# Score matmuls over whole 128-key chunks in 32x128 array tiles, barred squares cleared after the exponential, and a new order of the work

## The chip, the cores and the metric

The kernel runs on one core of a Trainium2 chip. A core has a matrix engine (TensorE, PE in the profile; PEld is its weight load), a vector engine (VectorE, DVE), a scalar engine (ScalarE, ACT), a general engine (GpSimd, POOL) and an engine for issuing transfers (SyncE, SP). Each engine works through its own list of instructions in order; semaphores order them against each other. The metric is device time in microseconds of one execution; lower is better.

## The reference

Attention with a block-causal mask, followed by one MLP-mixer layer. Inputs are q, k and v of shape (8, 8, 576, 64): eight batches, eight heads, 576 positions, head dimension 64. Cut to what matters:

```python
scores = scale * np.matmul(q, k.transpose(0, 1, 3, 2))
mask = block_i >= block_j                       # blocks of 64 positions
scores = np.where(mask, scores, -1000000000.0)
attn = softmax(scores)                          # over the keys
attn_out = np.matmul(attn, v)
x = attn_out.transpose(0, 2, 1, 3).reshape(B, S, 512)
h = np.maximum(x.transpose(0, 2, 1) @ w_tok1, 0.0) @ w_tok2     # over positions: 576 -> 256 -> 576
u = x + h.transpose(0, 2, 1)
h2 = np.maximum(u @ w_ch1, 0.0) @ w_ch2                         # over channels: 512 -> 1536 -> 512
out = u + h2
```

A query in block i sees the keys of blocks 0 to i, nine blocks of 64 in all. The kernel computes in bfloat16 with float32 accumulation.

## The kernel before, in words

**Scores.** Queries and keys are loaded as bfloat16 and transposed on VectorE as 32-bit pairs (line 442), so the 64 numbers of a head lie as two parities of 32 partitions. Four heads (a head group, `hg`) fill the 128 partitions, 32 each. A score matmul of one head therefore contracts over 32 rows, twice (`par` 0 and 1), and the array is used as tiles of 32 rows: four heads at once, one in each row group. Scores are made transposed, keys on the output partitions, queries along the columns. For each batch and head group there are three sets (`SETS`, emitted by `score_set`, matmuls at line 569), each of which fills one PSUM bank of 512 columns per head: set 0 holds key blocks 4 to 8, set 1 key blocks 2 and 3 and one square of blocks 0 and 1, set 2 the rest of blocks 0 and 1. Each entry of `SETS` is one matmul per head: (half of the output partitions, key block, first query block, first column, columns, parity). Before the change every matmul has 64 keys, so each row group holds two 32x64 tiles, one for each half of the partitions.

**The bar.** A chunk of 128 keys is two blocks. Queries of the first block may see the first 64 keys but not the second 64: a barred square of 64 keys by 64 queries. Before the change three of these squares (one in set 0, two in set 1) are written by a matmul of a constant tile `bar` (minus 2.5e8 times 1, entries with key block `None`), whose exponential is zero. Key block 8 stands alone and is copied to `et_sb` by `tail` (line 595); `tail` then clears the place that it left in `e_sb`, which is the barred square of blocks 6 and 7 (line 600).

**After the scores.** ScalarE takes the exponential of each bank into `e_sb` (line 776; lines 587 and 737 for batch 0). `head_out` (line 617) multiplies it with the values, which carry a column of ones for the sums; `ends_out` (line 670) does the last query block of two heads at a time in 128x64 tiles; VectorE divides. Then token mixing (lines 811, 815, 910; for batch 0 line 846), and the channel products up and down (1038 and 1460 for batch 0, 1111, 1235 and 1369 for the others, which trade matmuls for sums on VectorE). Results leave PSUM through VectorE or ScalarE (lines 395, 397, 797, 799, 925, 1393 and others).

**The order.** Each piece of work is an operation with a number, the number in which `Plan.add` was called. The constant `ORDER` lists all of them, in the order in which they are emitted; a letter names the engine (T TensorE, A ScalarE, D VectorE, P GpSimd, S SyncE), and small letters after T the PSUM banks that the operation takes. So each engine's list, the choice between VectorE and ScalarE or GpSimd, and the banks are all written out by hand; the costs given to `Plan.add` do not act here. GpSimd issues the loads (lines 419, 437, 471, 482, 505, 514) from the same list in which it copies and clears; SyncE issues the stores and the transposing loads of u (line 977).

**The start.** `raise_clock` issues 11 matmuls on zeros (line 366) and then small fillers on zeros (line 373) wherever `ORDER` names them; fillers that it does not name are not emitted. Batch 0's scores use two double banks (`sc`) that later become the four banks `late`.

Of the kernel before, what the change touches and what calls it, by code (L numbers as in the profile page):

```python
# [10 lines left out]
BF16 = mybir.dt.bfloat16  # L11
# [16 lines left out]
class Plan:  # L28
# [69 lines left out]
    16S 0A 11D 10D 13S 9D 21P 1D 2D 43Ta 5D 19P 4D 3D 23P 33P 27P 14A 25P 31P 15D 29P 17A 20D 37P 44Tb 45Tb 46Tb 22D  # L98
    47Ta 36P 48Ta 49Ta 18D 50Ta 51Ta 52Ta 35P 53Ta 24D 54Ta 55Ta 56Ta 125Ts 34P 100Ttbc 179P 126A 28D 57Ta 58Ta 59Ta
    176P 60Ta 61Ta 26D 62Ta 101A 12P 106Ts 63Ta 32D 182P 64Ta 107A 65Ta 104Tt 42P 30D 66Ta 67Ta 105A 68Ta 39P 123Ts  # L100
    102D 103D 69Ta 70Ta 41P 119A 71Ta 157Tt 124A 112Td 40P 113T 116Ta 108Tb 114D 120A 38P 109T 115D 138Ts 158A 181D
    81P 72Td 73Tc 74Tc 121D 75Tc 122D 139A 82P 76Tc 7D 144Tt 110D 111D 84P 135Td 178D 127Tc 145A 161Ts 185P 136D
    117D 137D 140D 131Tb 180D 83P 128T 162A 142Tt 177D 90P 132T 129D 143A 77Td 89P 163Ts 130D 133D 86P 134D 78Td
    164A 118D 141D 159D 200Tdcba 160D 85P 203A 173Te 154Tf 165Tg 202A 91P 174D 166T 155D 156D 201A 184D 92P 205Tbhfc
    204A 183D 169Td 88P 170T 209A 167D 263Ta 168D 208A 175D 150Tc 171D 261Tg 172D 207A 187D 267Td 206A 87P 186D
    146Te 262A 147T 264A 151T 268D 237Tgbfh 152D 339P 6D 148D 269Ta 153D 241A 149D 273Td 189P 240A 270D 281Tc 239A
    274D 265Te 190P 238A 271Ta 8D 282D 275Tb 266A 191P 193Tdhfg 276A 272D 283Te 196A 277Tc 342P 194A 315Ta 278D
    306Tb 197A 188P 294Td 195A 279Tc 284A 192P 318Tf 198D 280D 291Tg 319T 348P 316T 309Tc 317A 310T 257D 93P 320A
    307T 295T 94P 308A 292T 311A 258D 225Teahf 345P 296A 300Tb 227A 95P 285Tc 228A 286T 293D 226A 303Td 287D 229A
    304T 351P 232Tahge 341D 199D 312Tc 230D 233A 305D 313T 234A 231D 288Tf 344D 314A 297Ta 340D 236A 289T 343D 235A  # L110
    210Td 513P 245Tc 290A 211D 213Th 516P 212D 242Te 246D 216Tg 354P 247D 301T 214D 215D 248Td 243D 302A 298T 244D
    355P 217D 219Tc 249D 299A 250D 222Th 220D 254Te 221D 363Tdbaf 255D 256D 251Tc 349D 364A 330Te 352P 252D 365A
    218D 253D 321Td 367A 223D 224D 366A 259D 353P 368Tcghb 420Ta 372A 370A 422Tb 347D 371A 525P 346D 322T 421D 423A
    260D 369A 356Tafgh 323T 359A 357A 350D 424Tb 360A 324D 331T 358A 425D 388Tcadg 361P 514D 430Tb 391A 434Th 332T
    389A 431D 435A 518D 426Td 392A 517D 400Thcbf 390A 515D 428Tg 404A 393P 362D 334Ta 522P 403A 429D 677P 401A 335T
    333D 402A 528P 427D 376Tb 373Tc 394D 527P 96D 395Tdfgh 379Te 526P 377D 396A 374D 336T 375D 397A 519P 378D 380D
    405Tc 398A 680P 381D 382Tb 399A 406D 385Td 407D 432Te 337D 417Tc 383D 386D 433A 530Tafgh 387D 384D 418D 436Td
    419D 531A 440Tb 97D 414Tc 534A 325Te 533A 98D 326T 532A 415D 437A 416D 542Tahgf 99D 441A 438Tc 545A 327T 439D
    544A 444D 463Tgd 543A 445D 448Thb 328D 466A 464Tc 451D 546A 329S 411Ta 408Te 465A 446D 469T 412D 690P 413D 449Tf
    523D 470A 454T 529P 450A 409D 442Ta 410D 452Tc 455A 443D 691P 467Tg 520D 453A 537Taefh 447D 692P 468A 456T 521D  # L120
    538A 473T 689P 524D 539A 471T 679D 540A 683P 596Ta 457D 541A 474D 562Tcefh 597A 678D 458T 566A 681D 594Ta 565A
    459D 564A 460D 476T 563A 595D 461T 477A 569Tchfe 682D 462A 472D 604Ta 847P 571A 478Tdb 475D 686P 572A 605D 602Tg
    535P 481A 600Th 603D 536P 570A 598Ta 567P 482Tf 601D 607S 568P 553Tc 844P 599D 483A 479Tg 550Th 554D 555D 480A
    488T 551D 484T 552D 606S 489D 486T 485A 556Tc 487D 491T 573A 574Thadg 557D 490D 492A 547Te 558D 577A 493D 497Tbf
    575A 548D 576A 549D 559Tc 578A 688D 701Tedah 498A 685D 579Tg 560D 704A 684D 499T 705A 494D 850P 702A 693P 580D
    585Ta 703A 581D 503T 500D 687D 706Tgdbh 586D 587D 561D 591Te 504D 710A 501Ta 709A 495D 708A 592D 707A 593D 582Tc
    502D 627Tbd 612The 608D 630A 588Tg 583D 496D 505T 859P 615D 858P 633T 584D 506D 507T 857P 634A 589D 590D 860P
    694Tcgab 508D 856P 618T 698A 849D 509T 697A 846D 696A 619D 695A 760Tb 609D 610D 699P 510D 738Tacgh 761A 848D
# [42 lines left out]
    1457D 1392D 1492The 1453D 1393T 1488D 1493A 1489D 1455D 1498T 1394D 1458T 1396S 1460T 1490D 1459D 1472Tca 1468D  # L171
    1465S 1461D 1494T 1464S 1473A 1469D 1476Td 1470D 1478T 1491D 1462T 1479D 1471D 1499D 1482T 1463D 1496Tg 1477D
    1466S 1483D 1502T 1467S 1497D 1484T 1503D 1500T 1507S 1485D 1495D 1480T 1487S 1501D 1474T 1506S 1481D 1504T
    1475D 1486S 1505D 1508S
"""


@with_exitstack
def kernel(
# [340 lines left out]

    BARRED = 2.5e8

# [1057 lines left out]
```

## Time and profile before

| | |
|---|---|
| median of three runs | 284.23 us (284.23 to 285.07) |
| the profiled execution's own time (its span; the page gives no other) | 284.7 us |
| TensorE busy, instructions | 275.8 us, 4038 matmuls |
| VectorE, ScalarE, GpSimd busy | 240.3, 180.4, 71.7 us |
| instructions of line 569: loads of keys, loads of the bar | 1280, 192 |

In the profile a line names the engine, the source line and the operation, what is written and read, and the shape. For matmuls the shape begins with the array tile (rows * columns). TensorE's matmuls are pipelined: a matmul's listed duration includes its way through the array, and the next one starts before it ends, so what a matmul costs is the distance to the next start. A time in brackets is the engine's idle time before the instruction, with what ended it; "issue" means that nothing the profile shows was waited for.

### The profile page before, as it was taken

Reading aid. Unit: us, or ns where it says so; the run is one execution under the profiler, and the core shown is the slowest. Engines: PE = TensorE matmul, PEld = TensorE weight load, DVE = VectorE, ACT = ScalarE, POOL = GpSimd, SP = SyncE. Lnnn points to the kernel's source line nnn. Section 1 sums busy time; section 2 is a strip of 40 time slices with the busy share of each in tenths; the row PEclk is TensorE's granted clock in tenths of the full one; section 3 lists DMA queues with packets and bytes.
Section 4 is the critical chain, followed back from the end, with each engine's and each line's share of the span. In section 5 each row is a group of like instructions: output and inputs, shape, how many; then the busy total and the mean of one; then the engine's idle time right before and its main releaser. Section 6 shows DMA issues by size and latency. Waiting matters only on the chain.

```text
span 284.7 us, 9438 instructions
## 1 busy us (share of the span) xinstructions
PE 275.8 (97%) x4038; PEld 197.6 (69%) x4038; DVE 240.3 (84%) x519; ACT 180.4 (63%) x325; POOL 71.7 (25%) x120
## 2 busy tenths in 40 slices
PE   7998999999999899999999999999999999999994
PEld 3667656556878676987777658744488876468883
DVE  3589569799999799999998997997998987598893
ACT  3798685778888358996879785136546653764000
POOL 8975635170641062060341220000000000000000
PEclk9999999999999999999999999999999999999999
DMA  8999999969989495898199587130033403000246
GB/s 160 166 174 202 190 205 203 137 94 134 144 120 119 71 84 87 225 135 122 11 169 102 87 106 132 49 119 18 2 74 98 126 7 131 12 2 0 104 127 212
DMA packets 64776, 31.79 MB, mean 112 GB/s; under 512 B 53088, under 2 KB 55904, under 8 KB 64736
## 3 DMA queue, kind: packets, MB, share of 16 engines
q0 software_dynamic: 45040, 17.64, 53.1%
q1 hardware_dynamic: 19696, 13.57, 19.6%
q8 instruction: 31, 0.51, 0.7%
q14 instruction: 9, 0.07, 0.1%
HBM read 35.85 MB, written 9.44 MB: 159 GB/s over the span
## 4 chain that ended last, share of the span: by engine, by line
PE 92%; DVE 2%; ACT 2%; DMA 1%; issue 1%; SPq 0%; DVEq 0%
PE late L1369 14%; PE mm L1369 11%; PE late L1235 7%; PE mm L1111 7%; PE late L1111 6%; PE mm L569 6%; PE mm L1235 6%; PE mm L617 4%; PE mm L811 3%; PE mm L910 3%; PE mm L1038 3%; PE late L569 2%; PE late L617 2%; PE late L811 2%; PE mm L1460 2%; PE late L1460 2%
## 5 line engine op out<-in xcount | busy, mean ns | idle before, releaser
L776 ACT ACTIVATE e_sb<-late 128x512 bf16<-128x512 f32 x89 | 50.5, 609 | 10.4 <-PE late L569 9.1
L776 ACT ACTIVATE e_sb<-mm 128x512 bf16<-128x512 f32 x79 | 45.1, 609 | 9.9 <-PE late L569 6.6
L471 POOL DMA_DIRECT2D vals<-in_v_dram x45 | 37.2, 844 | 26.7 <-PE late L617 15.9
L442 DVE STREAM_TRANSPOSE qk_sb<-qk_sb 128x288 int32<-128x288 int32 (+2 forms) x57 | 36.2, 694 | 4.6 <-ACT qk_sb L395 3.5
L1369 PEld LDWEIGHTS <-sums 128*128 128x128 bf16 x288 | 27.6, 98 | 5.6 <-issue 1.8
L1369 PEld LDWEIGHTS <-gT 128*128 128x128 bf16 x288 | 27.8, 98 | 4.6
L569 PEld LDWEIGHTS <-qk_sb 32*64 32x64 bf16 x1280 | 19.9, 104 | 13.1 <-issue 8.8
L569 PE MATMUL mm<-qk_sb 32*64 32x64 bf16 (+7 forms) x546 | 27.8, 291 | 0.0
L569 PE MATMUL late<-qk_sb 32*64 32x512 bf16 (+7 forms) x594 | 27.1, 291 | 0.0
L617 PEld LDWEIGHTS <-e_sb 128*128 128x128 bf16 x640 | 23.8, 97 | 4.1 <-issue 0.9
L1111 PEld LDWEIGHTS <-ws_sb 128*128 128x128 bf16 x192 | 17.8, 98 | 3.4 <-issue 1.3
L797 ACT ACTIVATE gT<-mm 128x512 bf16<-128x512 f32 x25 | 14.7, 601 | 7.8 <-PE mm L1111 3.0
L617 PE MATMUL mm<-vals,e_sb 128*128 128x65 bf16 x430 | 19.0, 193 | 0.0
L643 DVE TENSOR_TENSOR x_sb<-mm,rinv 128x256 bf16<-128x256 f32 x43 | 17.9, 421 | 1.1
L1111 PEld LDWEIGHTS <-wc_sb 128*128 128x128 bf16 x144 | 15.4, 114 | 1.8 <-issue 0.2
L1235 PEld LDWEIGHTS <-ws_sb 128*128 128x128 bf16 x96 | 9.3, 98 | 10.1 <-issue 0.2
L1369 PE MATMUL late<-wd_sb,sums 128*128 128x256 bf16 x108 | 13.6, 272 | 1.2 <-issue 1.2
L1369 PE MATMUL late<-wd_sb,gT 128*128 128x256 bf16 x120 | 14.7, 273 | 0.0
L595 POOL COPY vals<-e_sb 128x256 bf16<-128x256 bf16 x10 | 4.1, 412 | 40.9 <-issue 22.9
L395 ACT COPY mm<-late 128x512 f32<-128x512 f32 x17 | 9.9, 584 | 7.1 <-PE late L1235 5.0
L797 ACT ACTIVATE gT<-late 128x512 bf16<-128x512 f32 x17 | 10.2, 602 | 6.3 <-PE late L1235 3.4
L1235 PE MATMUL late<-e_sb,ws_sb 128*128 128x512 bf16 x44 | 12.6, 379 | 0.0
(203 smaller groups left out, 656.2 us busy)
## 6 DMA issues: line engine op xcount, KB each, us to landing
out_dram<-o_sb SPq DMA_DIRECT2D x14, 512.0 KB, 3.1
vals<-in_v_dram POOLq DMA_DIRECT2D x28, 128.0 KB, 5.4
qk_sb<-in_k_dram POOLq DMA_DIRECT2D x12, 288.0 KB, 6.3
qk_sb<-in_q_dram POOLq DMA_DIRECT2D x12, 288.0 KB, 5.9
out_dram<-o_sb SPq DMA_DIRECT2D x7, 256.0 KB, 3.2
wc_sb<-in_moe_w_ch_dram POOLq DMA_DIRECT2D x8, 192.0 KB, 7.7
wc_sb<-in_moe_w_ch_dram POOLq DMA_DIRECT2D x3, 512.0 KB, 10.4
vals<-in_v_dram POOLq DMA_DIRECT2D x15, 64.0 KB, 4.9
```

The lines of the kernel that those rows point to most:

```text
L442: nc.vector.transpose(dst[:, 0:S, :] .rearrange("p s e -> p (s e)") .bitcast(I32) .rearrange("p (a k) -> p k a", k=NB)[:, k0:k1], raw2.bit ...
L471: nc.gpsimd.dma_start(out=t[128 - p : 128, J, hs, 0:64], in_=src)
L569: nc.tensor.matmul(out=home(n)[64 * half : 64 * half + 64, c : c + w], lhsT=bar[r, 0] if j is None else kT[i][r, 64 * j : 64 * j + 64, par ...
L617: nc.tensor.matmul(out=u[:, I, 0:65], lhsT=e[:, h, c : c + 128], rhs=vt[:, J, head, 0:65], start=(J == 0), stop=(J == I),)
L643: nc.vector.tensor_tensor(out=xt[:, 0:4, 64 * head : 64 * head + 64], in0=u[:, :, 0:64], in1=ri[:, 0:4].to_broadcast([128, 4, 64]), op=MULT,)
L776: nc.scalar.activation(dst, bank_of(x), EXP, scale=scale)
L797: nc.scalar.activation(dst, src, RELU)
L811: nc.tensor.matmul(out=ps, lhsT=w1_sb[:, c, tt : tt + 255 : 2], rhs=xt[:, c, cols], start=(c == 0), stop=False)
L1111: nc.tensor.matmul(out=bank_of(bank)[:, 256 * o_ : 256 * o_ + 256], lhsT=x(o_, m), rhs=y[:, :, m, :], start=opens, stop=m == 1, skip_group ...
L1235: nc.tensor.matmul(out=bank_of(bank), lhsT=x(m), rhs=y[:, :, m, :], start=first and m == 0, stop=m == 1, skip_group_check=not first,)
L1369: nc.tensor.matmul(out=bank_of(bank)[:, 256 * i : 256 * i + 256], lhsT=x[:, kk, 128 * i : 128 * i + 128], rhs=y[:, kk], start=first and i ...
L1460: nc.tensor.matmul(out=ps, lhsT=gT[0][:, cc, 128 * si : 128 * si + 128], rhs=wc2_sb[:, cc, :], start=cc == 0, stop=cc == NDC - 1,)
```

## The change

1. Sets 1 and 2 use whole chunks of 128 keys: entries with half `None` write all 128 partitions, in 32x128 tiles. A set of four heads has 16 matmuls for 32 (set 1) and 8 for 16 (set 2).
2. Set 0 keeps 32x64 tiles. Its wide pair now has the same 320 columns for key blocks 4 and 5 and its parts change places; 40 matmuls for 44.
3. The tile `bar`, its two memsets and its matmuls go. The barred squares come out as real scores, and their exponentials are zeroed: `clear` sets two squares of 64 keys by 64 queries to zero with one memset, for set 0 (there one of the two is the place that `tail` left, as before) and for set 1. `head_out` and `ends_out` wait for the clears. There are 36 clears for 18.
4. The fillers of `raise_clock` become 512 columns wide, every fourth 256; 28 are in the order, for 35.
5. `ORDER` is new throughout, and with it banks and engines; the first loads on GpSimd and SyncE keep their places among each other.

```diff
 ORDER = """
-    16S 0A 11D 10D 13S 9D 21P 1D 2D 43Ta 5D 19P 4D 3D 23P 33P 27P 14A 25P 31P 15D 29P 17A 20D 37P 44Tb 45Tb 46Tb 22D
...
+    7D 5D 14S 19P 41Ta 17P 48Tb 3D 21P 58Tb 31P 25P 23P 29P 27P 53Tb 51Tb 0A 15A 6D 11S 35P 56Tb 12A 74Tb 55Tb 2D 9D
...
-    bar = sb.tile([128, 2, 64], BF16, name="bar")
...
-        fill("DVE", "bar", -1e5 + 1, (bar[:, 0, :], -BARRED), (bar[:, 1, :], 1.0))
...
         for n in range(KEEP):
             bank = {"covers": False}
-
-            def emit(o, bank=bank):
+            w = 512 if n % 4 else 256
+
+            def emit(o, bank=bank, w=w):
                 nc.tensor.matmul(
-                    out=bank_of(bank)[:, 0:256], lhsT=zeros[:, 0:128], rhs=zeros[:, 0:256],
-                    start=True, stop=True,
+                    out=bank_of(bank)[:, 0:w], lhsT=zeros[:, 0:128], rhs=zeros[:, 0:w], start=True, stop=True,
                 )
...
-    BARRED = 2.5e8
     SETS = (
         (
-            (0, 4, 4, 0, 320, 0), (1, None, 0, 0, 64, 0), (1, 5, 5, 64, 256, 0),
-            (0, 4, 4, 0, 320, 1), (1, 5, 5, 64, 256, 1),
-            (0, 6, 6, 320, 192, 0), (1, 8, 8, 320, 64, 0), (1, 7, 7, 384, 128, 0),
-            (0, 6, 6, 320, 192, 1), (1, 8, 8, 320, 64, 1), (1, 7, 7, 384, 128, 1),
+            (0, 4, 4, 192, 320, 0), (1, 5, 4, 192, 320, 0), (0, 4, 4, 192, 320, 1), (1, 5, 4, 192, 320, 1),
+            (0, 6, 6, 0, 192, 0), (1, 8, 8, 0, 64, 0), (1, 7, 7, 64, 128, 0),
+            (0, 6, 6, 0, 192, 1), (1, 8, 8, 0, 64, 1), (1, 7, 7, 64, 128, 1),
         ),
         (
-            (0, 2, 2, 0, 448, 0), (1, None, 0, 0, 64, 0), (1, 3, 3, 64, 384, 0),
-            (0, 2, 2, 0, 448, 1), (1, 3, 3, 64, 384, 1),
-            (0, 0, 0, 448, 64, 0), (1, None, 0, 448, 64, 0), (0, 0, 0, 448, 64, 1),
+            (None, 2, 2, 0, 448, 0), (None, 2, 2, 0, 448, 1), (None, 0, 0, 448, 64, 0), (None, 0, 0, 448, 64, 1),
         ),
         (
-            (0, 0, 1, 0, 512, 0), (1, 1, 1, 0, 512, 0), (0, 0, 1, 0, 512, 1), (1, 1, 1, 0, 512, 1),
+            (None, 0, 1, 0, 512, 0), (None, 0, 1, 0, 512, 1),
         ),
     )
     SCOL = (1024, 0, 512)
-    ECOL = (448, 0, 1024, 1344)
-    TAIL = 1344
+    ECOL = (448, 0, 1216, 1024)
+    TAIL = 1024
+    BARRED = ((1024, 192), (0, 448))
...
+                rows, keys = (slice(0, 128), 128) if half is None else (slice(64 * half, 64 * half + 64), 64)
...
-                        out=home(n)[64 * half : 64 * half + 64, c : c + w],
-                        lhsT=bar[r, 0] if j is None else kT[i][r, 64 * j : 64 * j + 64, par],
-                        rhs=bar[r, 1] if j is None else qT[i][r, 64 * q : 64 * q + w, par],
+                        out=home(n)[rows, c : c + w],
+                        lhsT=kT[i][r, 64 * j : 64 * j + keys, par],
+                        rhs=qT[i][r, 64 * q : 64 * q + w, par],
...
-        def emit_clear(o):
-            (nc.vector if o.engine == "DVE" else nc.gpsimd).memset(e[64:128, hs, TAIL : TAIL + 64], 0.0)
-
-        return copied, P.add(
-            TAILS, {"DVE": 0.12 if urgent else 0.17, "POOL": 0.32}, emit_clear, [copied], prio, urgent=urgent
+        return copied, clear(0, hg, hs, [copied], prio, urgent)
+
+    def clear(n, hg, hs, deps, prio, urgent=0):
+        c0, step = BARRED[n]
+        late_keys = e_sb[hg][64:128, hs, c0 : c0 + 2 * step].rearrange("p h (a c) -> p h a c", a=2)[:, :, :, 0:64]
+
+        def emit(o):
+            (nc.vector if o.engine == "DVE" else nc.gpsimd).memset(late_keys, 0.0)
+
+        return P.add(
+            TAILS, {"DVE": 0.17 if urgent else 0.24, "POOL": 0.5}, emit, deps, prio, urgent=urgent
         )
...
+                elif n == 1:
+                    these = [clear(1, hg, hs, these, prio + 0.1, urgent=1)]
...
+                elif s == 1:
+                    these = [clear(1, hg, slice(0, 4), these, prio + 0.1)] * 4
```

More of the change, by code (lines that the diff above doesn't have):

```diff
@@ L103 @@
[L103 to L112, printed above, removed]
@@ L578, in score_set @@
         op = P.add(
-            "PE", 0.48, emit, deps + pads["bar"], prio, take=notes, mode=1, urgent=2 * (b == 0),
+            "PE", 0.48, emit, deps, prio, take=notes, mode=1, urgent=2 * (b == 0),
         )
```

144 lines of the change are left out of this document (77 added, 67 removed).

## The prediction

> **What bounds the kernel now.** I read the page first, for the shares and the chain that ended last.
>
> ```profile
> span 284.7 us, 9438 instructions
> PE 275.8 (97%) x4038; PEld 197.6 (69%) x4038; DVE 240.3 (84%) x519; ACT 180.4 (63%) x325; POOL 71.7 (25%) x120
> PE   7998999999999899999999999999999999999994
> PE 92%; DVE 2%; ACT 2%; DMA 1%; issue 1%; SPq 0%; DVEq 0%
> ```
>
> TensorE carries 92% of the chain and is full in every slice but the first and the last few. Busy time of pipelined matmuls flatters, so next come two stretches (PE, PEld, DVE, ACT, POOL, clock) and then TensorE's timeline, where I compare starts, not durations.
>
> ```profile
> 20.81:30.00 9.19, 8.44 (x218) 7.00 (x219) 7.73 (x23) 7.57 (x16) 5.74 (x9) 1.00 1.14 202
> 100.00:180.00 80.00, 79.69 (x1587) 60.70 (x1586) 73.78 (x176) 61.60 (x118) 22.21 (x37) 1.00 0.81 112
> ```
>
> The clock is 1.00. What TensorE loses lies in two places: the start, and three holes later.
>
> ```profile
> 8.29 0.42 PE L569 MATMUL sc<-qk_sb 32*64 32x512 bf16 x6 [0.54 <-DVE qk_sb L442]
> 8.98 3.84 ACT L587 ACTIVATE e_sb<-sc 128x1024 bf16<-128x1024 f32 x4 [2.54 <-PE sc L569]
> 16.70 4.05 ACT L587 ACTIVATE e_sb<-sc 128x1024 bf16<-128x1024 f32 x4 [0.15 <-PE sc L569]
> 20.81 0.32 PE L670 MATMUL late<-vals,e_sb 128*64 128x65 bf16 x8 [0.20 <-ACT e_sb L587]
> ```
>
> Until 20.81 us the start hangs on the first keys and queries (scores from 8.29) and then on ScalarE, which makes batch 0's exponentials nearly without pause from 8.98 to 20.75. From 20.81 on TensorE has work all the time, except here:
>
> ```profile
> 27.49 0.19 PE L815 MATMUL late<-x_sb,w_sb 128*128 128x64 bf16 x1
> 28.43 0.20 PE L815 MATMUL late<-x_sb,w1o_sb 128*128 128x64 bf16 x1 [0.75 <-issue]
> ...
> 92.09 1.04 PE L1369 MATMUL late<-wd_sb,sums 128*128 128x256 bf16 x8
> 94.37 0.60 PE L1369 MATMUL late<-wd_sb,sums 128*128 128x256 bf16 x4 [1.24 <-issue]
> ...
> 148.44 0.59 PE L811 MATMUL mm<-x_sb,w_sb 128*128 128x512 bf16 x2 [0.31 <-DVE x_sb L643]
> ...
> q8 instruction: 31, 0.51, 0.7%
> ```
>
> From 27.49 to 28.43, and from the last of the eight (92.85) to 94.37, TensorE stood in the middle of a group and waited for no engine: 0.91 + 1.41 = 2.3 us beyond the slots of 0.03 and 0.11. The instruction queue fetches 31 times; I take the two holes for fetches that came late. Only the third, 0.3 us, is a wait for another engine. So the time is the gate at 20.81, plus all of TensorE's work after it, plus holes, plus an end that both kernels have alike (last group of six matmuls, one addition, one store).
>
> **The change, part by part.** *Score sets.* These rows show where one set of each kind begins and where the next work begins; then the slots of 512- and 256-column matmuls, and the weight loads of the first set.
>
> ```profile
> 132.60 0.93 PE L1369 MATMUL late<-wc_sb,gT 128*128 128x256 bf16 x7
> 133.46 0.41 PE L569 MATMUL mm<-qk_sb 32*64 32x512 bf16 x3
> ...
> 133.71 0.39 PE L569 MATMUL mm<-qk_sb 32*64 32x512 bf16 x3
> ...
> 133.73 0.38 PE L569 MATMUL late<-qk_sb 32*64 32x512 bf16 x1
> 134.05 0.61 PE L1111 MATMUL late<-uT,ws_sb 128*128 128x256 bf16 x4
> 134.49 0.27 PE L1369 MATMUL late<-wd_sb,sums 128*128 128x256 bf16 x1
> ...
> 138.97 0.39 PE L569 MATMUL mm<-qk_sb 32*64 32x448 bf16 x3
> ...
> 139.43 0.19 PE L569 MATMUL late<-qk_sb 32*64 32x64 bf16 x1
> 139.55 0.22 PE L670 MATMUL late<-vals,e_sb 128*64 128x65 bf16 x2
> ...
> 117.83 0.33 PE L569 MATMUL mm<-qk_sb 32*64 32x320 bf16 x2
> ...
> 118.45 0.39 PE L1111 MATMUL mm<-th_sb,ws_sb 128*128 128x256 bf16 x2
> ```
>
> ```profile
> 58.76 1.73 PE mm L1460 x8
> 207.83 6.55 PE late L1369 x60
> ```
>
> ```profile
> 133.45 0.16 PEld L569 LDWEIGHTS <-qk_sb 32*64 32x64 bf16 x16 [0.21 <-issue]
> ```
>
> Set 2 takes 0.59 us, set 1 0.58, set 0 0.62. A slot is 0.216 us for 512 columns (1.73/8) and 0.109 for 256 (6.55/60). In set 2 each tile streams twice 512 columns, 0.43; the remaining 0.16 is the first weights (second batch at +0.25, not +0.216: 0.035), the stagger of eight tiles (133.71 to 133.73: 0.02) and the way out (133.73 + 0.216 to 134.05: 0.10). The way in costs 0.10 too (seventh slot of 132.60 ends at 133.36, the set begins at 133.46). A 128x128 group that begins after a set pays only 0.01 for its first weights: 134.05 to 134.49 is 0.44 for four slots of 0.109.
>
> A 32x128 tile takes both halves of a chunk, so the columns per row group stay 1024 and the stream stays 0.43. What goes is half of the instructions (16 to 8 in set 2, 32 to 16 in set 1, both bars among them) and half of the stagger. Its first weights are 128 wide as in the 128x128 rows, so I take 0.01 instead of 0.035: set 2 becomes 0.55, set 1 0.55 (448 + 448 + 64 + 64 columns are the same 0.43). Set 0 keeps 32x64 tiles but has 40 matmuls for 44 and even columns in both halves: 0.60. Per pair of batch and head group 0.04 + 0.03 + 0.02; after the gate 14 such triples: **-1.2 us**. From both sides: the stream and the way out stay, so no set goes under 0.53 and the gain stays under 14 x (0.06 + 0.05 + 0.09) = 2.8; a loss is the first rival below.
>
> *What is done at the gate.* Counted through the two orders from the group that waits at 20.81: before, 41 sets, 600 matmuls of line 617 and 300 of line 670 remain, with 98 changes of array shape; after, 42 sets, 580, 290 and 102. By these rows
>
> ```profile
> 60.49 0.60 PE mm L617 x20
> ...
> 63.55 0.44 PE mm L670 x20
> ```
>
> that is +0.45 (a set without its way out), -0.60, -0.22, +0.40: **0.0**. The first set is now one of 40 matmuls instead of 8, so ScalarE starts later: the last matmul of a set 0 begins some 0.45 after the first and lasts 0.22, 8.29 + 0.45 + 0.22 + 0.05 = 9.01 to 9.03 for 8.98: **+0.05**. The fillers (28 for 35, most of them 512 wide) lie ahead of the gate and cost nothing; without that cover, half a filler, 0.1. Two memsets less on VectorE at the start are hidden by its wait for the first keys.
>
> *Fetches.* 455 matmuls and their loads fewer (448 of scores, 7 fillers) are 910 of 8076 instructions of TensorE, so about 28 fetches for 31, and the sets eat instructions half as fast. From 0 to -2.3; I take one hole in two: **-1.15**.
>
> *The new order.* TensorE has no slack, so a new order can only add waits. What a result needs to come back shows here (group, then the copy it releases):
>
> ```profile
> 237.31 0.59 PE L1235 MATMUL late<-e_sb,ws_sb 128*128 128x512 bf16 x2
> ...
> 237.94 0.57 ACT L395 COPY late<-late 128x512 f32<-128x512 f32 x1 [0.24 <-PE late L1235]
> ```
>
> The slots of the two end at 237.74; the copy starts 0.20 later and lasts 0.57; TensorE takes it up about 0.05 later (20.81 against ScalarE's end at 20.75): 0.82. Two groups of two 512-column matmuls in between give 0.86. Adding up TensorE's work between each group and the nearest group whose evacuated result or bank it needs, I find 2 places under 0.1 us of margin in the old order and 32 in the new. The old order's one negative margin is the wait at 148.44, so the measure says something. A place costs nothing if its engine is free and up to 0.29 (half a copy) if one is in front: 0 to 9 us. Nearest are the old order's places of 0.1 to 0.25, which wait nowhere; I take 0.03 each: **+0.9**.
>
> *Clears and queues.* One clear more per head group (18), and a set's clear is twice as large.
>
> ```profile
> L595 POOL COPY vals<-e_sb 128x256 bf16<-128x256 bf16 x10 | 4.1, 412 | 40.9 <-issue 22.9 <-ACT e_sb L776 17.9
> L600 POOL MEMSET e_sb<- 64x256 bf16 x9 | 2.8, 306 | 5.6 <-PE mm L910 5.2
> ```
>
> At double size I take 0.5 on GpSimd; 23 of 36 go there, 13 to VectorE. Behind each stand GpSimd's loads: a tail of 0.41 and two clears of 0.31 now lie ahead of the second token weights and the channel weights, so these issue up to 1 us later. The shortest way from a later load's issue to its first use by TensorE is 12 us of TensorE work in the new order, 10 in the old: hidden. ScalarE's and VectorE's sums change by under 3 us, beside TensorE. On SyncE two stores stand ahead of batch 3's transposing loads (line 977), whose times to landing are:
>
> ```profile
> DMA to landing us min/median/max: 3.0/3.5/10.6
> ```
>
> From the result they wait for to their first use the new order leaves 7.9 us (batch 2) and 6.2 (batch 3), the old 12.8 and 10.1; a usual one needs 0.2 + 0.7 + 3.5. Hidden at the median, priced at 0; with 10.6 it is a rival.
>
> **Sum.** -1.2 + 0.05 - 1.15 + 0.9 = -1.4. The profiled span of 284.7 lies 0.5 over the runs' median of 284.23; taken off the median: 282.8 us.
>
> **Rivals.**
> 1. *Weights not hidden (slower).* If a row group's next weights can't load while it streams, a lane of 32x128 tiles pays about 0.1 us at one further load in set 2 and three in set 1: 14 x 0.4 = 5.6 in place of 14 x 0.07 = 1.0 gained. 284.23 + 5.6 - 0.3 + 0.05 - 1.15 + 0.9 = 289.3. It decides once 0.1 us is paid per triple. Against it: all 16 loads of the set at 133.45 were done by 133.61, eight of them under matmuls of the same row groups. Chance 0.05. The Trainium skill, TensorE: Matmul & The Clock Gate, section Part 3: Packing small matmuls, says that LDWEIGHTS overlaps with in-flight MATMULs only when the row group differs. By that rule this rival would be the forecast; the trace does not agree.
> 2. *The order's tight places are caught (slower).* 12 of the 32 find a copy in front, 12 x 0.29 = 3.5 in place of 0.9: 285.4. It outweighs the rest from 8 places on. For it: the margins; against: the old order ran the same engines without waits. Chance 0.20.
> 3. *A transposing load lands late (slower).* One of 10.6 us, 0.9 before it: 11.5 - 7.9 = 3.6 us at batch 2's channel work: 286.4. Decides at 9 us. Against: GpSimd issues no load around it in the new order. Chance 0.10.
> 4. *No gain that can be told.* 32x128 sets take as long as before, or both fetch holes stay: 284.0. Chance 0.17.
>
> **How the numbers follow.** Forecast 0.48, with 281.3 to 283.3 of its own (both holes gone and no tight place caught; or one of them not). The range takes in rivals 2 to 4, 281.3 to 286.4, and leaves out rival 1 and about 0.1 at its ends. A measurement tells about 0.3% (0.85 us) from no change: faster 0.48, same 0.17 (rival 4), slower 0.35 (rivals 1 to 3).
>
> **What would show it.** In the timeline, 32x128 sets of 0.55 us and set 0 at 0.60; the gate at 20.8 to 20.9; one hole of about 1 us with "issue" or none; waits of TensorE for ScalarE or VectorE after 30 us below 1 us in sum. The prediction is wrong if a 32x128 set takes over 0.6, if TensorE waits for banks by more than 2 us, or if the gate moves past 21.5.

## The result and the profile after

The changed kernel is slower by 0.6%: 286.40 us at the median of five runs (286.02 to 286.67) against 284.55 (284.23 to 285.07) of the kernel before, a ratio of 1.0063 (95% interval 1.0039 to 1.0088). 282.8 was forecast. A few executions in the experiments below ran over 1.5% longer than the rest of their kernel, and the ratios leave them out. The page of the changed kernel:

```profile
span 284.8 us, 8573 instructions
PE 278.0 (98%) x3583; PEld 194.8 (68%) x3583; DVE 239.0 (84%) x519; ACT 177.0 (62%) x327; POOL 80.4 (28%) x134
PE   8999999999999999999999999999999999999993
q8 instruction: 28, 0.46, 0.6%
q10 hardware_dynamic: 144, 0.26, 0.2%
PE 79%; DMA 8%; POOL 5%; DVE 2%; ACT 2%; issue 2%; POOLq 0%; ACTq 0%
```

910 instructions of TensorE are gone and the instruction queue fetches 28 times for 31. Yet the span (the time from the first instruction to the last) is 284.8, as the profiled one of before (284.7), and the chain now passes through DMA and GpSimd. In the timeline, first a set 2 and its weights, then the start:

```profile
127.80 0.12 PEld L562 LDWEIGHTS <-qk_sb 32*128 32x128 bf16 x8 [0.21 <-issue]
127.81 0.40 PE L562 MATMUL mm<-qk_sb 32*128 32x512 bf16 x3
...
128.37 1.05 PE L1114 MATMUL late<-uT,ws_sb 128*128 128x256 bf16 x8
```

```profile
8.54 1.96 ACT L580 ACTIVATE e_sb<-sc 128x1024 bf16<-128x1024 f32 x2 [3.35 <-PE sc L562]
...
18.75 2.07 ACT L580 ACTIVATE e_sb<-sc 128x1024 bf16<-128x1024 f32 x2 [0.56 <-PE sc L562]
...
20.75 0.27 PE L372 MATMUL mm<-wd_sb 128*128 128x256 bf16 x1
20.86 0.37 PE L616 MATMUL mm<-vals,e_sb 128*128 128x65 bf16 x7
```

The set takes 0.56 us, its eight loads are done in 0.12. TensorE's work behind its last filler begins at 20.86. No hole with "issue" is left in TensorE's timeline. Instead it waits (timelines of GpSimd, TensorE, its weight loads and VectorE):

```profile
25.79 0.53 POOL L503 DMA_DIRECT2D wc_sb<-in_moe_w_ch_dram  x1 [1.94 <-DMA w_sb<-in_moe_w_tok_dram]
...
33.70 0.36 PEld L1041 LDWEIGHTS <-wc_sb 128*128 128x128 bf16 x3 [0.62 <-DMA wc_sb<-in_moe_w_ch_dram]
...
41.22 1.06 PEld L616 LDWEIGHTS <-e_sb 128*128 128x128 bf16 x28 [0.22 <-DVE e_sb L599]
...
43.26 0.35 PE L562 MATMUL mm<-qk_sb 32*128 32x448 bf16 x1 [0.21 <-DVE x_sb L642]
...
128.52 1.59 DVE L1168 TENSOR_SCALAR gT<-gT 128x1024 bf16<-128x1024 bf16 x2
...
130.03 0.67 DVE L1153 TENSOR_TENSOR gT<-late,half 128x512 bf16<-128x512 f32 x1
...
130.75 0.60 PE L1114 MATMUL late<-th_sb,wc_sb 128*128 128x256 bf16 x4 [0.46 <-DVE gT L1153]
...
170.95 0.46 PE L616 MATMUL late<-vals,e_sb 128*128 128x65 bf16 x10 [0.17 <-DVE x_sb L642]
```

By TensorE's starts the waits that end at 33.70, 41.22, 43.26, 130.75 and 170.95 cost 0.31 us (33.18 to 33.70, less a slot), 0.27, 0.28, 0.63 and 0.34, and one at 29.84, for a copy on VectorE, another 0.26. The first is for the load that GpSimd issues at 25.79, all others are for VectorE.

**The profile of before was not a usual execution.** Each run of the comparisons has its time and its span. For the changed kernel and for before:

```
after,  5 runs: time 286.02 to 286.67, span 284.2 to 284.8, time less span 1.80 to 1.96
before, 33 runs (beside the first four experiments): time 283.96 to 288.20,
        span 282.2 to 286.4 (median 283.4), time less span 1.73 to 1.83
```

In all of these some 1.8 us lie outside the span. So the execution of before with a span of 284.7 took about 286.5 us (284.7 + 1.8; its own time isn't known), 2.3 over the median of 284.23 that the prediction set it against. It was longer than usual by just about its two holes (0.91 + 1.41). Here is before once more, unchanged.

> The kernel before, unchanged, profiled once more. Theory: a run's time is its span plus 1.8 us, so the execution shown in the prediction (span 284.7) was one of about 286.5 us, over 2 us slower than the timed runs; its holes of 0.91 and 1.41 us with nothing to wait for are not a part of every execution. This look then has a span of 282.2 to 284 and as much less hole in TensorE as its span is under 284.7. Rival: the holes are fixed places of the order, both are there again at the same instructions, and the span is 284.5 or more.

Measured: 284.53 us, span 282.8, so 1.73 outside.

```profile
span 282.8 us, 9438 instructions
q8 instruction: 31, 0.51, 0.7%
PE 93%; DVE 2%; DMA 2%; ACT 1%; issue 1%; POOL 0%; DVEq 0%; POOLq 0%
```

The two holes are not there; elsewhere are two of 0.21 (21.43) and 0.29 us (146.41). The wait for the last exponential of batch 0, the prediction's gate, ends at 20.74:

```profile
20.74 0.32 PE L670 MATMUL late<-vals,e_sb 128*64 128x65 bf16 x8 [0.32 <-ACT e_sb L587]
```

With this trace the two kernels can be set side by side. I sorted the distance from each TensorE start to the next: nominal slots of 128-row shapes, score sets up to the next other work, changes of shape, what is over by less than 0.06 us, and what is over by more (waits and holes).

```
us                                  before again   after    more
until work behind the last filler       19.76      20.86    1.10
slots behind it                        232.40     231.71   -0.69
score sets                              25.84      24.75   -1.09
changes of shape (56, 60)                5.29       5.71    0.42
under 0.06 us each                      -5.83      -5.36    0.47
waits and holes                          0.84       2.57    1.73
last start to the end of the span        4.50       4.55    0.05
sum (span 282.8, 284.8)                                     2.0
```

The waits take 1.7 us more, the small losses 0.5. (The row under 0.06 us is negative because some short matmuls follow each other faster than their nominal slot.) Two sets hold waits. The first set of before, at 19.76, ends at the gate and takes 0.98 us for 0.58, so 0.4 of the sets' gain is the same 0.4 that the start seems to lose (1.10 less the 0.69 of work already done by then). And one set after, at 22.97, holds a wait of 0.26 (a matmul at 23.26, behind a product on VectorE that ends at 23.21). Without both the sets gain 0.95 (25.44 to 24.49).

### The profile page after: what moved, and what is told of

Same layout as the page of the kernel before. It is cut to its first block, busy times and chain, and to the rows that moved or that the text cites. A ratio compares the mean times of both kernels' runs of the same rounds, so it can differ in the third digit from the quotient of the medians.

```text
span 284.8 us, 8573 instructions
## 1 busy us (share of the span) xinstructions
PE 278.0 (98%) x3583; PEld 194.8 (68%) x3583; DVE 239.0 (84%) x519; ACT 177.0 (62%) x327; POOL 80.4 (28%) x134
## 4 chain that ended last, share of the span: by engine, by line
PE 79%; DMA 8%; POOL 5%; DVE 2%; ACT 2%; issue 2%; POOLq 0%; ACTq 0%
PE mm L1372 13%; PE late L1372 13%; PE mm L1114 8%; PE mm L1238 7%; PE late L1238 6%; PE late L1114 5%; PE late L1463 4%; PE late L562 3%; PE mm L562 3%; DMA wc_sb<-in_moe_w_ch_dram 3%; PE late L616 3%; DMA qk_sb<-in_q_dram 3%; PE late L814 3%; PE mm L616 2%; PE late L913 2%
## 5 line engine op out<-in xcount | busy, mean ns | idle before, releaser
L777 ACT ACTIVATE e_sb<-mm 128x512 bf16<-128x512 f32 x93 | 53.0, 613 | 15.2 <-PE mm L562 9.1
L562 PE MATMUL mm<-qk_sb 32*64 32x320 bf16 (+6 forms) x546 | 28.0, 272 | 0.2 <-DVE x_sb L642 0.2
L562 PEld LDWEIGHTS <-qk_sb 32*64 32x64 bf16 (+1 forms) x1024 | 17.3, 99 | 14.8 <-issue 8.9
L562 PE MATMUL late<-qk_sb 32*128 32x64 bf16 (+6 forms) x370 | 26.4, 278 | 0.0
L393 ACT COPY late<-mm 128x512 f32<-128x512 f32 x16 | 9.2, 581 | 18.1 <-PE mm L1238 11.4
L599 POOL MEMSET e_sb<- 64x512 bf16 (+1 forms) x23 | 11.6, 509 | 30.0 <-ACT e_sb L777 15.6
L616 PE MATMUL late<-vals,e_sb 128*128 128x65 bf16 x310 | 14.1, 193 | 0.2 <-DVE x_sb L642 0.2
L580 ACT ACTIVATE e_sb<-sc 128x1024 bf16<-128x1024 f32 x11 | 10.8, 1041 | 4.1 <-PE sc L562 4.1
L814 PE MATMUL late<-x_sb,w_sb 128*128 128x512 bf16 (+1 forms) x68 | 13.3, 323 | 0.0
L642 DVE TENSOR_TENSOR x_sb<-late,rinv 128x256 bf16<-128x256 f32 x31 | 12.8, 417 | 0.6
```

The source lines that it names most:

```text
L562: nc.tensor.matmul(out=home(n)[rows, c : c + w], lhsT=kT[i][r, 64 * j : 64 * j + keys, par], rhs=qT[i][r, 64 * q : 64 * q + w, par], start ...
L599: (nc.vector if o.engine == "DVE" else nc.gpsimd).memset(late_keys, 0.0)
L616: nc.tensor.matmul(out=u[:, I, 0:65], lhsT=e[:, h, c : c + 128], rhs=vt[:, J, head, 0:65], start=(J == 0), stop=(J == I),)
L642: nc.vector.tensor_tensor(out=xt[:, 0:4, 64 * head : 64 * head + 64], in0=u[:, :, 0:64], in1=ri[:, 0:4].to_broadcast([128, 4, 64]), op=MULT,)
L777: nc.scalar.activation(dst, bank_of(x), EXP, scale=scale)
L814: nc.tensor.matmul(out=ps, lhsT=w1_sb[:, c, tt : tt + 255 : 2], rhs=xt[:, c, cols], start=(c == 0), stop=False)
```

## Experiments

Ratios are to runs of the kernel before on the same chip, with their 95% interval. The medians of those runs lie between 284.76 and 285.22 us, so medians of different experiments can be compared only to within some 0.5 us.

**A second store queue.** The page shows a new queue, q10, for one store that ScalarE issues. My first theory was that it costs the 1.8 us outside the span, which I took before not to have. The edits: `1522A` becomes `1522S` in the changed kernel; in the kernel before `1487S` becomes `1487A`, and `676S 842S 843S` become `676A 842A 843A`.

> The kernel after with one word changed: store 1522 is issued by SyncE as all others are, and no longer by ScalarE. Theory A (the 1.8 to 1.9 us that the changed kernel's time has over its span, where before has none, are the price of the second hardware DMA queue, which this one store opens): 284.5 us (284.2 to 284.9), span within 0.3 us of 284.8, time less span under 0.3 us. Rival B (the time outside the span comes from the start, or from anything else in the new order): 286.4 us as after, and still 1.8 us beside the span. Rival C (the store issued by SyncE comes later, because 1523, 1502 and 1503 are issued by the same engine): the span grows by 0.3 to 1.0 us.

> The kernel before with one late store of 256 KB or less, 1487, issued by ScalarE instead of SyncE. Theory A (a second hardware DMA queue costs a fixed time outside the span): 286.4 us (286.0 to 286.8), span 284.7 as before or up to 0.4 less, 1.8 us beside the span. Rival B: 284.3 us, nothing beside the span.

> The kernel before with three stores of the middle (676, 842, 843, issued between 155 and 184 us) on ScalarE, all late ones on SyncE. Theory A, fixed price of the queue whenever it is used: 286.4 us, 1.8 us beside the span. Theory A2, a price for each store on that queue: 3 x 1.85 = 5.6 us beside the span, 290 us. Theory A3, the price is that of a late store whose completion is waited for at the end: nothing beside the span, 284.5 us. ScalarE's copies behind the three stores can come up to 1 us later; that would be seen in the span.

Measured: 286.99 us, 1.0061 (1.0032 to 1.0091); 285.02, 0.9985 (0.9960 to 1.0010); 284.51, 0.9973 (0.9946 to 1.0001). Time less span: 1.80 to 1.92, 1.85 to 2.07, 1.82 to 1.91. Theories A, A2 and A3 fall: about 1.8 us lie outside with that queue and without it. The queue costs 0.2 us at most: by medians 1.98 and 1.86 with it where before has 1.78, while the changed kernel without it has 1.84 for 1.87. What fills the 1.8 us isn't shown. The profiled execution of the first (span 286.6) had one late load besides:

```profile
20.98 0.57 PE L616 MATMUL mm<-vals,e_sb 128*128 128x65 bf16 x10 [1.50 <-DMA vals<-in_v_dram]
```

**Tiles without the new order.**

```
-            (0, 0, 1, 0, 512, 0), (1, 1, 1, 0, 512, 0), (0, 0, 1, 0, 512, 1), (1, 1, 1, 0, 512, 1),
+            (None, 0, 1, 0, 512, 0), (None, 0, 1, 0, 512, 1),
```

and set 1 likewise, without its bars and with nothing in their place.

> The kernel before, in its own order, with the scores of sets 1 and 2 alone in 32x128 tiles and set 0 as it was. It leaves out the barring of the squares of sets 1 and 2, with nothing in its place. What it tells is the gain of the tiles without the new order and without the clears: by the traces (set 2 from 590 to 564.5 ns, set 1 from 583 to 564 ns, 14 of each in the batches behind the first) 14 x 0.045 = 0.6 us, so 283.8 us (283.5 to 284.1) if TensorE's time is the end's time; 283.4 by the prediction's 0.55 us a set; 284.5 if the gain is swallowed by the next wait. If the two holes of 0.91 and 1.41 us in the trace of before are late instruction fetches they may move or go, as TensorE has fewer instructions here: then up to 2.3 us less.

Measured: 283.91 us, 0.9949 (0.9927 to 0.9972). In the old order the tiles gain. Median sets: set 2 0.562, set 1 0.565, set 0 still 0.616; the shorter sets make some 0.6 us. Its spans lie within 281.6 to 282.3 (median 281.8), those of before within 282.2 to 286.4 (283.4), and its trace has no hole over 0.2 us with "issue": part of the gain seems to be that holes are gone. Outside the span it has 2.1 us for 1.78, so the time gains 0.3 less than the span; why isn't shown.

**The new order without the tiles.** The changed kernel's order, renumbered, in the program of before.

> The program of the kernel before (32x64 tiles, barred squares as matmuls, one small clear a head group) put in the order of the changed kernel, the 18 clears of set 1 left out of it. Theory N: the order's waits stay (0.6 us near 130 us, where TensorE waits for VectorE), and the sets take the longer times of before, 0.9 to 1.2 us more; less 0.9 us for three waits that stand behind clears of set 1: span 284.2 to 285.5, time 286.0 to 287.5. Rival W: without the clears and the new layout the order runs as well as the old one: span 282.2 to 283.4, time 284.0 to 285.3.

Measured: 286.17 us, 1.0053 (1.0033 to 1.0073), spans from 283.8 (before beside it: from 282.1). So the order is slow with the old tiles as well, and without set 1's clears. Its profile (285.3) has three holes with "issue" (0.70, 0.51 and some 0.7 us by TensorE's starts), and near 130 us only 0.13 of the 0.6 expected; that part of N missed.

**Are the clears the cause?**

```
+            if n == 0:
                 (nc.vector if o.engine == "DVE" else nc.gpsimd).memset(late_keys, 0.0)
```

> The changed kernel in its own order, without the 18 clears of set 1; it leaves out the zeroing of set 1's barred squares. In the trace of the changed kernel VectorE has such a clear in front of the copy or the reciprocal that TensorE waits for at 29.84 (0.26 us), 40.92 (0.27) and 170.59 (0.34). If these clears are the cause, the three waits go: 0.9 us less, time 285.3 to 286.0. If the order alone leaves too little room, the waits stay in other places and the time is 286.4 to 287.

Measured: 286.41 us, 1.0055 (1.0034 to 1.0076): nothing gained. The waits at 29.8 and 41 us shrank to about 0.1, the one at 170 stayed at 0.34, and the one for the channel weights grew to 0.51:

```profile
33.88 0.58 PEld L1042 LDWEIGHTS <-wc_sb 128*128 128x128 bf16 x4 [0.82 <-DMA wc_sb<-in_moe_w_ch_dram]
```

**Are the wide fillers?** `w = 512 if n % 4 else 256` becomes `w = 256`.

> The changed kernel with fillers of 256 columns in all 28 places instead of 512 in 21 of them. The prediction priced the wide fillers at nothing. If they stand in the way of the first scores (ScalarE idle for 0.20 and 0.56 us ahead of 18.75 us, with a 0.22 us filler between the scores it waits for and the work before them): TensorE's work behind the last filler starts 0.3 to 0.6 us earlier, time 285.8 to 286.1. If they are hidden: no change, 286.2 to 286.7.

Measured: 286.53 us, 1.0051 (1.0028 to 1.0074). TensorE's work behind the last filler began at 20.50 for 20.86, as the first branch said, and the time did not follow. In the trace the weights' wait was 0.38 for 0.31, so only 0.07 of the 0.36 was given back there, and the profiled span is 0.7 shorter (284.1). So in this trace the wide fillers cost some 0.3 us at the start; the times and the other spans (284.0 to 285.8) don't show it. They are not what makes the order slow.

**Four waits mended.** Each operation of VectorE that stood ahead of the awaited one goes behind it (in the second pair the clear, which is awaited, goes ahead):

```
-207D 196A 285Te 280D      -348D 190P 201D      -632D 662D 920A 799T 800D      -1107D 1092Tf 1093D 1094D
+196A 285Te 280D 207D      +201D 348D 190P      +632D 920A 799T 800D 662D      +1092Tf 1093D 1094D 1107D
```

> The changed kernel with four operations of VectorE moved by one to three places in its own order: the clear ahead of the copy at 29.68, the transpose ahead of the clear at 40.89, one clip (0.86 us) ahead of the joined result at 130.03, the clear ahead of the reciprocal at 170.26. TensorE waited 0.26, 0.27, 0.63 and 0.34 us there. Theory N: the four waits go and the time with them, 1.5 us less than after: 284.6 to 285.4. Rival G (the room is short everywhere, a mended wait comes back as the next one): under 0.5 us less, 285.9 to 286.6.

Measured: 286.15 us, 1.0012 (0.9988 to 1.0037). The time fits rival G (0.25 less than after), the ratio fits N (0.63% over before has become 0.12%, and the intervals do not meet); the runs of before beside it had a median of 285.21 for 284.55. So part of the loss went with the four waits, and how much isn't settled. In the trace three of the four are gone or under 0.1; near 130 us TensorE now waits 0.55 for the next result, and at 33 us 0.96:

```profile
34.01 0.84 PE L1042 MATMUL late<-uT,wc_sb 128*128 128x512 bf16 x3 [0.80 <-DMA wc_sb<-in_moe_w_ch_dram]
...
131.48 0.38 PE L563 MATMUL late<-qk_sb 32*128 32x512 bf16 x1 [0.48 <-DVE gT L1154]
```

**The load at 33 us.** On GpSimd's queue the last of the second token weights stood behind a tail copy and a clear of batch 0, and the channel weights behind it. Added to the four moves: `160P 161P ... 81P` becomes `81P 160P 161P`.

> The changed kernel with the four moves on VectorE (e15, 286.15 us) and one more on GpSimd: the last load of the second token weights stands ahead of the tail copy and the clear of the first batch instead of behind them, so that it and the eight channel-weight loads behind it issue some 0.6 us earlier. Theory L (the wait of 0.96 us at 32.83 is set by this queue): the wait shrinks by 0.4 to 0.6 us and the time with it, 285.4 to 285.9. Rival (the loads are bound by what the DMA engines move, not by their issue): the weights land at 33.9 to 34.1 us as before, time 286.0 to 286.5.

Measured: 285.70 us, 1.0026 (1.0001 to 1.0051). GpSimd's timeline before and behind this move, then TensorE's behind it:

```profile
18.96 0.53 POOL L481 DMA_DIRECT2D w_sb<-in_moe_w_tok_dram  x1
...
25.48 0.53 POOL L504 DMA_DIRECT2D wc_sb<-in_moe_w_ch_dram  x1 [1.81 <-DMA w_sb<-in_moe_w_tok_dram]
```

```profile
18.82 0.55 POOL L481 DMA_DIRECT2D w_sb<-in_moe_w_tok_dram  x1
...
24.20 0.54 POOL L504 DMA_DIRECT2D wc_sb<-in_moe_w_ch_dram  x1 [0.46 <-DMA w_sb<-in_moe_w_tok_dram]
```

```profile
32.71 0.59 PE L1042 MATMUL mm<-uT,wc_sb 128*128 128x512 bf16 x2
33.14 1.46 PE L1042 MATMUL late<-uT,wc_sb 128*128 128x512 bf16 x6
```

The last channel weights wait for that token-weight load to land; they issue 1.28 us earlier, and TensorE goes on at 33.14 without a wait. The median is 0.45 us under the one with the four moves alone, within what L gave; but the ratio is not lower (1.0026 for 1.0012, intervals overlapping), and the fastest spans are alike (283.5 and 283.4). So L is borne out in this trace and not in the time. Even in the trace the token-weight load itself issued just 0.14 us earlier, because the one ahead of it waited 0.50 for a landing in this execution; the rest is that GpSimd could go on 5.4 us after it for 6.5. How much of the wait the queue's order makes, and how much the spread of the landings, is not settled.

**Other ways to bar, and late fetches.** Set 2 alone in tiles; sets 1 and 2 in tiles with the bars added behind, `+ (1, None, 0, 0, 64, 0), (1, None, 0, 448, 64, 0),`.

> The kernel before with the scores of set 2 alone (which has no barred square) in 32x128 tiles: complete, in the old order, without any clear more. Theory N (TensorE is the bound of the old order, so what a set saves comes out at the end): 14 sets x 0.026 us and two of the start, -0.4 us, and as TensorE has 128 matmuls fewer perhaps less in late fetches: 0.1 to 0.5% under before. Rival (any gain ends in another wait): within 0.1% of before.

> The kernel before, in its own order, with sets 1 and 2 in 32x128 tiles, and set 1's two barred squares added onto the scores by 32x64 matmuls behind them, as they were barred before; complete, no clear more. With the tiles alone (without bars) the time was 0.5% under before. If a step from 32x128 to 32x64 tiles inside a set is free: 0.3 to 0.5% under before. If it costs 0.1 us as other changes of shape do: 14 x 0.1 = 1.4 us more, 0 to 0.2% above before.

Measured: 286.01 us, 1.0026 (1.0007 to 1.0044), and 287.49, 1.0082 (1.0054 to 1.0110). Of the second, TensorE's timeline of one set 1:

```profile
91.17 0.36 PE L569 MATMUL late<-qk_sb 32*128 32x448 bf16 x1
...
91.74 0.21 PE L569 MATMUL late<-bar 32*64 32x64 bf16 x1
...
91.92 0.45 PE L617 MATMUL late<-vals,e_sb 128*128 128x65 bf16 x9
```

0.75 us for 0.565: the step to 32x64 tiles and eight small matmuls together cost 0.18 a set, 2.6 us for 14. The first was slower than before although its sets 2 took 0.563; its trace has a hole:

```profile
64.25 0.25 PE L570 MATMUL late<-qk_sb 32*64 32x192 bf16 x3
66.03 0.21 PE L570 MATMUL late<-qk_sb 32*64 32x64 bf16 x2 [1.53 <-issue]
```

The trace dates the packets of the instruction queue. The ten holes of over 0.2 us that lie inside a group or a set and show no engine as their cause (gaps of one matmul slot, where a record is missing, are left out):

```
            last fetch begins    hole ends    later by
before         25.99, 92.02    28.43, 94.37   2.44, 2.35
before again   144.49          146.91         2.42
old order, one late store on ScalarE  91.57   93.82   2.25
new order, old tiles  20.05, 26.56, 161.35    22.38, 28.85, 163.95   2.33, 2.29, 2.60
set 2 alone    63.52           66.03          2.51
bars added     28.26           30.67          2.41
batch 0 with bars (last kernel below)  92.36  94.79   2.43
```

In all ten TensorE goes on 2.25 to 2.60 us after a fetch began, whatever it was doing. So I read these holes as fetches that began too late. Two more, of 0.23 and 0.34 us, do not fit (3.1 and 4.4 us behind the last fetch); the first stands where other traces show a wait for VectorE. Whether the holes hang on the place in the instruction stream alone was tried with the 11 warm-up matmuls of 512 columns split into 22 of 256, once with set 2 in tiles and once in the kernel before.

> The kernel before with set 2 in 32x128 tiles (e8, 286.0 us, with a hole of 1.70 us at 64.26 that follows the fetch of 63.52) and its 11 warm-up matmuls of 512 columns split into 22 of 256: the same time ahead of the first score, 11 matmuls and 11 weight loads more. Theory F (the hole is a fetch that comes too late for the place it serves): all later fetches fall some 22 instructions earlier in the work, the hole at 64 us goes or moves, time 284.0 to 285.2. Rival (the hole is a fixed place of that program): hole and time stay, 285.7 to 286.4.

> The kernel before with the same split of its warm-up matmuls, nothing else. Theory F: the places of the late fetches change, so the spread of the runs and the median change by 0.3 us or more either way (284.0 to 284.8, or over 285.6); the fastest runs, which have no hole, stay at 283.8 to 284.0. Rival: median as before within 0.2 us.

Measured: 285.50 us, 1.0002 (0.9978 to 1.0025), and 285.47, 1.0007 (0.9982 to 1.0032). By time the first is 0.5 faster than unshifted (on another chip, intervals overlapping), neither 1.7 nor nothing; the second cannot be told from before. The trace says more, though it is of one execution of 291.3 us, 5.8 over the median. The weight loads behind the hole, in the set at 64 us, unshifted and shifted:

```profile
66.04 0.22 PEld L570 LDWEIGHTS <-qk_sb 32*64 32x64 bf16 x17 [1.80 <-issue]
```

```profile
65.88 0.35 PEld L572 LDWEIGHTS <-qk_sb 32*64 32x64 bf16 x28 [0.96 <-issue]
```

The hole is in the same set of 44 loads, once behind the 27th and once behind the 16th: eleven earlier, as many as the split put in. It ends 2.54 us after a fetch that began at 63.34, an eleventh case. So the hole kept its place in the instruction stream and moved in the work, as theory F has it. What makes a fetch begin late stays open.

**The changed program in the old order.** Every operation at its old place, the 18 new clears inserted; first behind their exponentials, then with narrow fillers and the clears late, then with `144D 164D` moved behind `117D`.

> The changed program (32x128 tiles, new layout, all 36 clears) put in the order of the kernel before: each operation at its old place and on its old engine, the 18 new clears behind the exponentials that they follow (13 on GpSimd, 5 on VectorE), and sets 1 and 2 exchanged in five places so that a clear has time. Theory N (the new order is what costs): no waits as in the changed kernel, span 281.6 to 282.6 as with the tiles alone, time 283.6 to 284.5, 0.3 to 0.5% under before. Rival W (the program itself costs: clears, layout, shape changes): span 283.5 to 285, time 285.3 to 287, with waits for the clears or for what stands behind them on VectorE and GpSimd.

> The changed program in the order of the kernel before once more, with two faults of the first try mended: its fillers were 512 columns wide in 35 places that had 256 (fillers took 9.80 us for 7.05, and TensorE's work behind the last of them began at 22.49 us for 19.76), and clears stood right behind their exponentials, where VectorE and GpSimd waited for ScalarE with other work queued behind. Here all fillers have 256 columns and a clear stands only some 2.6 us of TensorE's work ahead of its first use, on GpSimd but for the first batch. Theory N: work behind the last filler from 19.7 to 20.1 us, span 281.7 to 282.8, time 283.6 to 284.6. Rival W (clears of this size find no room in the old order either): span over 283.5, time over 285.3.

> The changed program in the old order (e10) with two clears of the first batch moved behind three reciprocals and products on VectorE, where the first try had them wait 0.69 us for ScalarE with the bank TensorE needs behind them (the set at 19.38 us took 2.05 us for 0.97). Theory N: that set back to about 1.0 us, span 1.0 us less than e10 (283.4 to 285.2): 282.2 to 283.6, time 284.1 to 285.4. Rival W: the time is lost to the next clear and stays at 286 to 287.

Measured: 288.58 us, 1.0128 (1.0104 to 1.0152); 286.63, 1.0041 (1.0019 to 1.0063); 285.04, 0.9980 (0.9958 to 1.0003). The third differs from the second by the place of two clears of batch 0 alone: in the second, VectorE waits in a clear, and the bank that TensorE needs is read behind it.

```profile
19.39 0.31 DVE L600 MEMSET e_sb<- 64x128 uint32 x2 [0.69 <-ACT e_sb L581]
...
20.20 0.35 PE L563 MATMUL mm<-qk_sb 32*128 32x448 bf16 x1 [0.46 <-DVE x_sb L643]
```

**A version under both.** Batch 0 as in the kernel before; from batch 1 on sets 1 and 2 in tiles, 14 clears late on GpSimd:

```
-            for half, j, q, c, w, par in SETS[s]:
+            for half, j, q, c, w, par in (WHOLE if b else SETS)[s]:
...
+                elif s == 1:
+                    these = [clear(hg, these, prio + 0.1)] * 4
```

> The kernel before, in its own order: batch 0 as it was, with bars; from batch 1 on sets 1 and 2 in 32x128 tiles, with 14 clears of set 1's squares on GpSimd, some 2.6 us of TensorE's work ahead of their use, and sets 1 and 2 exchanged in five places. Theory N (the tiles' gain of 0.6 us comes out in an order that keeps its room): TensorE's work behind the last filler from 19.7 to 20.1 us, fastest runs 283.4 to 283.8, median 284.0 to 284.8, 0.1 to 0.5% under before. Rival W (clears and late fetches take it): 285.0 to 286.0.

Measured: 284.43 us, 0.9971 (0.9946 to 0.9996), spans from 281.6. Work behind the last filler begins at 19.62. It is complete, and 2.0 us under the changed kernel's 286.40 (beside other runs of before). Theory N holds, by a small margin; its profiled execution (span 283.5) has the hole of the table's last row.

## Why the prediction was wrong

Here are the terms of the sum, counted as the prediction counted them, from the gate (20.74 in before once more, 20.86 after):

```
us                      forecast   measured
score sets                -1.2       -0.95
gate                      +0.05      +0.12
work behind the gate       0.0       +0.3
fetches                   -1.15       0
the new order             +0.9       +2.5
sum                       -1.4       +2.0
```

The forecast for the order is the new waits, and the fetches are the holes that were to go. The measured column is the table of the two kernels with the two waits taken out of the sets. The work is -0.69 of slots, +0.58 for one set more and +0.42 of changes of shape; another 0.05 lies at the end of the span. The order is 1.73 + 0.26 of waits and 0.47 of small losses.

1. *The base of the sum and the fetches (-1.15).* In the order of the sum this step failed first: "The profiled span of 284.7 lies 0.5 over the runs' median of 284.23; taken off the median". Span and time differ by some 1.8 us in the runs of before, so the profiled execution lay 2.3 over the median, and its two holes were hardly in the time that they were subtracted from. That late fetches make the holes is borne out (2.25 to 2.60 us in eleven cases), and the changed kernel's trace has none. But the term had to be priced against the median, where no more than some tenths were to be had on the first chip: its runs of before had spans of 282.4 to 283.3 (time less 1.8), and the shortest span of any run of before is 282.0.
2. *The new order (+0.9).* This is the larger miss: 2.5 us came. The price of 0.03 at each tight place had no row behind it; the nearest places of the old order waited nowhere. What came was not a little at each of 32 places but 0.26 to 0.63 at seven, six of them for VectorE as far as the trace tells. The sign "waits of TensorE for ScalarE or VectorE after 30 us below 1 us in sum" was missed: 0.27, 0.28, 0.63 and 0.34 are 1.52. That the order is the cause, and not the tiles or the clears, is shown: with the old tiles it is as slow (1.0053), without set 1's clears too (1.0055), and the changed program in the old order is no slower than before (0.9980), once two clears of batch 0 stand late enough (1.0041 without that). The mechanism was of the kind of rival 2 (a result one operation too far behind on its engine). Rival 2's size is another matter: it reckoned 12 places and 3.5 us, and that its 285.4 with the 1.15 of the fetches put back comes to 286.5 is partly luck.
3. *Clears and queues (0).* Wrong at one place: "hidden" was derived from 12 us between issue and use. The channel weights' last load issued at 25.79, after GpSimd had stood 1.94 us until earlier weights landed, and was awaited until 33.70, 7.9 us. Whether the copy and the clear ahead of the loads make the wait isn't shown: in before once more that load issued at 25.37, just 0.42 earlier. With the four waits mended it issued at 25.48, and TensorE still waited until 34.01.
4. *Score sets (-1.2).* Right in kind: 0.564 us for 0.55 (both 32x128 sets), 0.600 for 0.60. By the medians a triple saved 0.025 + 0.019 + 0.017 for 0.09, 0.85 us; the step that was off is the first weights, taken as 0.01 and measured as 0.024 (second batch at +0.24, not +0.216).
5. *Gate (+0.05), work behind it (0.0) and fillers (nothing).* The gate came at 20.86, within the 20.8 to 20.9 named. The slots and changes of shape behind it came nearly as counted (-0.69 for -0.82, +0.42 for +0.40). The fillers did cost: with narrow ones the work behind them began 0.36 earlier in the trace, though the time did not fall.
6. *Rivals 1 and 3* did not come: no set is longer, and no wait of TensorE for a transposing load is in the list of waits. The Trainium skill (TensorE: Matmul & The Clock Gate, Part 3: Packing small matmuls) says that weight loads overlap matmuls in flight only when the row group differs. This trace does not agree: in 32x128 tiles the eight loads of a set, two for each row group, were done 0.12 us after the set began, while its first four matmuls take 0.216 us to stream.

The signs named for a wrong prediction (a set over 0.6, the gate past 21.5) watched the terms that held; none watched the base.

## What to carry to other kernels

Before subtracting a hole from a time, look whether the profiled execution is a usual one: compare span with span, and take a second profile. In an order without slack, a shorter piece of work buys only what the next wait leaves: in the old order the tiles were worth 0.5% without any bar and 0.3% in a complete kernel, in the new one nothing (1.0063 with them and the clears, 1.0053 without). And a load is hidden only if its landing, here 7.9 us, ends before its use; distance in work alone doesn't show that.

## What was unexpected

The tiles alone (0.9949) and set 2 alone (1.0026) lie 0.8% apart, although the second does half of the first's edit: its trace has a hole of 1.70 us after a late fetch. One change of tile shape inside a set, with eight small matmuls behind it, cost 0.18 us, more than the whole gain of the tiles in that set (0.02). And 1.72 to 2.51 us lie outside the span in the runs here; by medians that differs by up to 0.35 from kernel to kernel (1.77 to 2.12), and why isn't shown.
